# Later loads for the fifth and sixth groups and a new hand-written order in an mLSTM, SoLU and top-1 expert kernel

## The chip, the cores and the metric

The kernel runs on one core of one Trainium2 chip. The metric is the device time of one execution in microseconds (us), lower is better.

## The reference

Three stages follow each other on 4 x 768 = 3072 tokens of 320 numbers. First a gated recurrence (mLSTM, 8 heads of 40), then a layer `x @ w_in`, a softmax-weighted activation, a layer norm and `@ w_out`, then one of 8 experts for each token.

```python
for t in range(S):                                   # stage 1, per batch and head
    m_new = np.maximum(f_gate[:, :, t] + m, i_gate[:, :, t])
    C = f_stab * C + i_stab * einsum('bhd,bhe->bhde', vt, kt)
    n = f_stab * n + i_stab * kt
    y[:, :, t] = sigmoid(o_gate) * (C @ qt) / max(|n @ qt|, 1)
h = x @ w_in; e = np.exp(h - h.max(-1)); solu = h * e / e.sum(-1)    # stage 2
x = layernorm(solu) * g_ln @ w_out
idx = argmax(normalize(x) @ normalize(expert_emb).T / tau)           # stage 3
out = gate * (relu(x @ w1[idx]) @ w2[idx])
```

## The kernel before

The tokens are cut into 24 groups of 128 (6 chunks for each of 4 batches). The recurrence is computed by chunks: for each group the scores of queries and keys (`smat`, L626), their product with the values (`pv`, L637), the part carried over from the chunks before (`inter`, L642) and the new state (`smm`, L647). Then follow for each group the gate (`den`, `og`, L654 to L662), the transpose of x (`xtr`, L671), the first layer (`mm1`, L686 to L695), the softmax (`negmax` L699, `expo` L704, `umul` L709), transposes of u (`utr`, L732), the second layer (`mm2`, L748 to L750) and the row for routing.

Products in full precision are made from two rounded halves, so each weight matrix is split on the core into a high and a low part. `w_in` and `w_out` come as 64-bit numbers and are decoded on VectorE first (`dec_in`, `dec_out`, three instructions each, L397 to L399). ScalarE writes the high part (`whi`, L421 and L424; `ohi`, L566), VectorE the low part (`wlo`, L428; `olo`, L569). This decoding, the gates' running maxima (`gmax0` L348, `gsum0` L358, with TensorE's `gls0` L356 and `gx0` L365 around them), the embeddings' product with `w_out` (`wtr` L525, `ep` L538, which gives the routing scores as extra columns of `w_out`) and the first three groups' attention make up the opening, some 48 us. The raw weights share four slots (`raw`), so the third and the fourth fetch of `w_in` wait until the two decodings of `w_out` have freed theirs. Ten pairs of products without use (`fill`, L600) write into the bank `H`, the same that `gls0` writes and `gsum0` reads.

Routing goes by blocks of up to four groups: place in the expert (`pos`, L810), a key (`key`), two one-hot tables for each group made on GpSimd (`okr`, L837 and L839, for the last block on VectorE), and a product of them that inverts the permutation (`invm`, L845). From the inverted table VectorE works out the rows to gather (`col_0` for the two fullest experts, `col_2` and `col_4` for the others, L1037 to L1041). GpSimd gathers the rows of an expert (`xg`, L1118), TensorE transposes them (`xt`, L1129), and the two layers of the expert follow (`m1`, L1157 to L1161; `m2`, L1208 to L1210).

Nothing is scheduled at run time. Every step is entered into a plan with its engine and with what it needs, and a table of numbers (`AT`) gives each step its place: the steps are sorted by their numbers and written out in that order, so each engine's instructions, and SyncE's loads, stand in it. The numbers only order. Loads of queries and keys (`load_q`, L605, 4 buffers) and of keys, values and gates (`load_n`, L612, 4 buffers) are steps of SyncE; at first they wait for nothing but their buffer. ScalarE applies tanh to each group's gates as soon as its own order comes to it (`tprep`, L618), and GpSimd scales the values (`vprep`, L615).

```python
keys = sorted(self.steps, key=at.get)
for k in plan.order():
    plan.steps[k]["fn"]()
```

Of the kernel before, what the change touches and what calls it, by code (L numbers as in the profile page):

```python
# [20 lines left out]
B, H, S, D = 4, 8, 768, 40  # L21
# [38 lines left out]
NFILL = 10  # L60
INP = ((0, 1), (1, 2), (2, 4), (4, 5))
# [157 lines left out]
def moe_kernel(ctx: ExitStack, tc: tile.TileContext, qkT, nat, gates, w_in, w_out, emb, w1, w2, cst, out):  # L219
# [73 lines left out]
    add = plan.add  # L293
# [777 lines left out]
    g = NG - 1  # L1071
# [498 lines left out]
```

## Time and profile before

| | us |
|---|---|
| three runs: median, lowest, highest | 524.79, 520.2, 525.45 |
| the profiled execution | 522.23 |
| its span, first to last instruction | 520.4 |
| TensorE busy in the span | 494.0 |
| VectorE, ScalarE, GpSimd busy | 340.0, 275.0, 203.9 |
| mean granted TensorE clock | 0.985 |

The profile lists, for each engine, when each instruction started, how long it took, how long the engine had been idle before it and which engine or transfer ended that idle time. Consecutive matmuls overlap in it, since a matmul's end is its last result; the distance from one start to the next is what a matmul costs. The granted clock is 1.00 at TensorE's upper level (2.4 GHz) and 0.50 at its lower (1.2 GHz).

### The profile page before, as it was taken

Reading aid. Unit: us, or ns where it says so; the run is one execution under the profiler, and the core shown is the slowest. Engines: PE = TensorE matmul, PEld = TensorE weight load, DVE = VectorE, ACT = ScalarE, POOL = GpSimd, SP = SyncE. Lnnn points to the kernel's source line nnn. Section 1 sums busy time; section 2 is a strip of 40 time slices with the busy share of each in tenths; the row PEclk is TensorE's granted clock in tenths of the full one; section 3 lists DMA queues with packets and bytes.
Section 4 is the critical chain, followed back from the end, with each engine's and each line's share of the span. In section 5 each row is a group of like instructions: output and inputs, shape, how many; then the busy total and the mean of one; then the engine's idle time right before and its main releaser. Section 6 shows DMA issues by size and latency. Waiting matters only on the chain. (4 is left out here: it accounts for less than half of the span.)

```text
span 520.4 us, 14487 instructions
## 1 busy us (share of the span) xinstructions
PE 494.0 (95%) x5925; PEld 452.2 (87%) x5925; DVE 340.0 (65%) x735; ACT 275.0 (53%) x604; POOL 203.9 (39%) x350
## 2 busy tenths in 40 slices
PE   6869999999999999999999899999999999999991
PEld 5747998888899999889898789898999999999991
DVE  5997667777677587677778778677463655485120
ACT  3572555665656556666467565554543644565220
POOL 3221223266246247345315683656172444112021
PEclk9989999999999999999999899999999999999996
DMA  8962233343341253414041412835631861563000
GB/s 300 412 223 81 80 83 120 113 147 111 90 144 46 77 156 121 144 40 143 3 171 44 152 47 96 276 84 193 231 92 44 285 223 64 217 189 121 14 21 31
DMA packets 20139, 68.01 MB, mean 131 GB/s; under 512 B 2658, under 2 KB 6050, under 8 KB 19680
## 3 DMA queue, kind: packets, MB, share of 16 engines
q1 hardware_dynamic: 17120, 58.27, 33.5%
q0 software_dynamic: 2944, 8.73, 5.3%
q8 instruction: 49, 0.80, 0.7%
q14 instruction: 26, 0.21, 0.1%
HBM read 58.31 MB, written 8.72 MB: 129 GB/s over the span
## 5 line engine op out<-in xcount | busy, mean ns | idle before, releaser
L1222 POOL DMA_INDIRECT out_x<-you,sidx x28 | 30.8, 1099 | 95.5 <-ACT you L1215 82.9
L748 PE MATMUL Y<-OH,uh 128*128 128x328 f32 x192 | 63.4, 330 | 0.0
L1190 DVE SCALAR_TENSOR_TENSOR lu<-hpu,uu 128x384 fp32r<-128x384 f32 (+4 forms) x56 | 28.6, 519 | 53.0 <-ACT uu L1184 43.5
L750 PE MATMUL Y<-OH,ul 128*128 128x328 f32 x192 | 60.3, 314 | 0.2 <-DVE ul L740 0.2
L749 PE MATMUL Y<-OL,uh 128*128 128x328 f32 x192 | 60.4, 315 | 0.0
L1208 PE MATMUL ypu<-hr,uu 128*128 128x320 f32 (+4 forms) x192 | 60.1, 313 | 0.0
L1209 PE MATMUL ypu<-lr,uu 128*128 128x320 f32 (+4 forms) x192 | 59.3, 309 | 0.0
L1184 ACT ACTIVATE uu<-hpu 128x384 fp32r<-128x384 f32 (+7 forms) x64 | 30.4, 483 | 52.2 <-PE hpu L1161 40.0
L1109 DVE TENSOR_TENSOR lr<-raw,hr 128x1024 fp32r<-128x1024 f32 (+1 forms) x32 | 43.4, 1355 | 15.1 <-ACT hr L1102 15.1
L1210 PE MATMUL ypu<-hr,lu 128*128 128x320 f32 (+4 forms) x168 | 51.8, 309 | 0.0
L1102 ACT CAST hr<-raw 128x1024 fp32r<-128x1024 f32 (+1 forms) x40 | 45.2, 1134 | 10.5 <-DMA raw<-in_w 9.4
L736 ACT CAST uh<-tpu 128x512 fp32r<-128x512 f32 x48 | 27.7, 586 | 38.7 <-PE tpu L732 38.4
L704 ACT ACTIVATE e<-H,nmx 128x1024 f32<-128x1024 f32 x24 | 26.8, 1117 | 40.2 <-DVE nmx L699 40.2
L1118 POOL DMA_INDIRECT xgr<-ys,gidx x28 | 36.5, 1302 | 27.3 <-issue 8.9
L699 DVE TENSOR_REDUCE nmx<-H 128x1 f32<-128x1024 f32 x24 | 29.4, 1224 | 26.1 <-PE H L695 24.5
L1157 PE MATMUL hpu<-exr,hr 128*128 128x384 f32 (+7 forms) x128 | 43.7, 341 | 0.0
L1158 PE MATMUL hpu<-exr,lr 128*128 128x384 f32 (+7 forms) x128 | 42.5, 332 | 0.0
L1159 PE MATMUL hpu<-exr,hr 128*128 128x384 f32 (+7 forms) x128 | 42.4, 332 | 0.0
L686 PE MATMUL H<-WH,xh 128*128 128x512 f32 x96 | 40.7, 424 | 1.2 <-DVE u L709 1.1
L740 DVE TENSOR_TENSOR ul<-tpu,uh 128x512 fp32r<-128x512 f32 x48 | 32.4, 687 | 12.6 <-ACT uh L736 12.5
L687 PE MATMUL H<-WL,xh 128*128 128x512 f32 x96 | 37.9, 395 | 0.1
L748 PEld LDWEIGHTS Y<-OH,uh 128*128 128x128 f32 x192 | 36.2, 189 | 2.0 <-ACT yr L766 0.2
(230 smaller groups left out, 1351.3 us busy)
## 6 DMA issues: line engine op xcount, KB each, us to landing
qk<-in_qkT SPq DMA_DIRECT2D x24, 512.0 KB, 4.2
raw<-in_w SPq DMA_DIRECT2D x24, 512.0 KB, 4.7
nat<-in_nat SPq DMA_DIRECT2D x24, 484.0 KB, 3.7
raw<-in_w SPq DMA_DIRECT2D x16, 640.0 KB, 5.3
ys<-yr SPq DMA_DIRECT2D x5, 772.0 KB, 5.0
raw<-in_w_out SPq DMA_DIRECT2D x2, 1280.0 KB, 9.3
raw<-in_w_in SPq DMA_DIRECT2D x3, 512.0 KB, 6.4
raw<-in_w_in SPq DMA_DIRECT2D x1, 1024.0 KB, 8.3
```

The lines of the kernel that those rows point to most:

```text
L686: T.matmul(out=o, lhsT=xh[:, kk, :], rhs=WH[:, kk, f], start=(kk == 0), stop=False)
L748: T.matmul(out=yp, lhsT=uh, rhs=OH[:, k, :], start=(k == 0), stop=False)
L749: T.matmul(out=yp, lhsT=uh, rhs=OL[:, k, :], start=False, stop=False)
L750: T.matmul(out=yp, lhsT=ul, rhs=OH[:, k, :], start=False, stop=(k == 7))
L1102: A.copy(out=R.h[i], in_=R.raw[i])
L1109: eng.tensor_tensor(out=R.l[i], in0=R.raw[i], in1=R.h[i].bitcast(F32), op=ALU.subtract)
L1157: T.matmul(out=o, lhsT=R.h[k][:, fs_], rhs=xh[:, k, tk], start=(k == 0), stop=False)
L1158: T.matmul(out=o, lhsT=R.l[k][:, fs_], rhs=xh[:, k, tk], start=False, stop=False)
L1159: T.matmul(out=o, lhsT=R.h[k][:, fs_], rhs=xl[:, k, tk], start=False, stop=False)
L1208: T.matmul(out=yp, lhsT=uh, rhs=hi, start=(f == 0), stop=False)
L1209: T.matmul(out=yp, lhsT=uh, rhs=lo, start=False, stop=False)
L1210: T.matmul(out=yp, lhsT=ul, rhs=hi, start=False, stop=(f == 7))
```

## The change

The four loads of the groups 4 and 5 (counted from 0) now come after `ep` 1, the second half of the embeddings' product with `w_out`. All numbers of the table are replaced, so that steps stand in a new order on every engine. The steps of the opening move most: the loads, GpSimd's memsets (`set_z` ahead of `sets`), a low part of `w_in`, the fills. Behind the opening most steps keep their neighbours or change places with one of them. No instruction is added or removed.

```diff
+LATER = (4, 5)
...
-    "load_q": "30 115 87 359 332 531 908 1069 ...",
+    "load_q": "30 97 80 345 714 694 903 1065 ...",
-    "col_2": "6816",
+    "col_2": "6550",
...
-        add(("load_q", g), "S", lambda g=g, s=s, q=q: load_q(s, qkT[g], q), war=[of("smat", g - nq), of("inter", g - nq)], size=524)
-        add(("load_n", g), "S", lambda g=g, s=s, q=q: load_n(s, nat[g], q), war=[("og", g - nn), of("smm", g - nn), of("pv", g - nn)], size=496)
+        add(("load_q", g), "S", lambda g=g, s=s, q=q: load_q(s, qkT[g], q), after=[("ep", 1)] if g in LATER else (), war=[of("smat", g - nq), of("inter", g - nq)], size=524)
+        add(("load_n", g), "S", lambda g=g, s=s, q=q: load_n(s, nat[g], q), after=[("ep", 1)] if g in LATER else (), war=[("og", g - nn), of("smm", g - nn), of("pv", g - nn)], size=496)
```

The line numbers of the changed kernel are one higher throughout.

**SyncE, the loads of the opening.** The number behind `qk` or `nat` is the group. Before, from the second fetch of `w_out` on:

```order
L392 DMA raw_66<-in_w_out 128x2560
L605 DMA qk4_260<-in_qkT 128x1024
L605 DMA qk3_270<-in_qkT 128x1024
L314 DMA cs_75<-in_cst 128x496
L612 DMA nat2_321<-in_nat 128x968
L392 DMA raw_66<-in_w_in 128x2048
L612 DMA nat4_431<-in_nat 128x968
L605 DMA qk5_469<-in_qkT 128x1024
L392 DMA raw_66<-in_w_in 128x1024
L612 DMA nat5_504<-in_nat 128x968
```

Now, from the same fetch on:

```order
L393 DMA raw_66<-in_w_out 128x2560
L613 DMA nat2_253<-in_nat 128x968
L606 DMA qk3_269<-in_qkT 128x1024
L613 DMA nat3_276<-in_nat 128x968
L393 DMA raw_66<-in_w_in 128x2048
L393 DMA raw_66<-in_w_in 128x1024
L606 DMA qk5_554<-in_qkT 128x1024
L613 DMA nat4_558<-in_nat 128x968
L606 DMA qk4_561<-in_qkT 128x1024
L613 DMA nat5_567<-in_nat 128x968
```

The four loads of the groups 4 and 5 moved behind the last fetch of `w_in`, and the constants' second part (`cs`) moved out of this stretch, ahead of the second fetch of `w_in`.

**VectorE and TensorE around the gates' second maximum.** VectorE before, from the end of the second decoding of `w_in` to the first decoding of `w_out`:

```order
L399 SCALAR_TENSOR_TENSOR wf0_210<-raw_66,wf0_210 128x512
L492 RECIPROCAL et_125<-et_125 8x1
L493 TENSOR_TENSOR et_125<-et_125,rtau_79 8x1
L358 SCALAR_TENSOR_TENSOR gx_118<-H0_161,z_119 32x767
L631 TENSOR_TENSOR Pt1_242<-S0_1_224,cs_75 128x512
L631 TENSOR_TENSOR Pt1_242<-S1_1_225,cs_75 128x512
L397 TENSOR_SCALAR of0_256<-raw_66 128x1280
```

Now:

```order
L400 SCALAR_TENSOR_TENSOR wf0_211<-raw_66,wf0_211 128x512
L493 RECIPROCAL et_125<-et_125 8x1
L494 TENSOR_TENSOR et_125<-et_125,rtau_79 8x1
L429 TENSOR_TENSOR WL_111<-wf0_211,WH_110 128x512
L359 SCALAR_TENSOR_TENSOR gx_118<-H0_160,z_119 32x767
L632 TENSOR_TENSOR Pt1_243<-S0_1_222,cs_75 128x512
L632 TENSOR_TENSOR Pt1_243<-S1_1_223,cs_75 128x512
L398 TENSOR_SCALAR of0_255<-raw_66 128x1280
```

A low part of `w_in` (L429), which stood behind the gate of group 1, now stands ahead of the maximum (L359). TensorE before, from the last scores of group 1 to the first values:

```order
L626 MATMUL S1_1_225<-qk1_179 128x128
L501 MATMUL tpe_236<-cs_75,en_124 128x8 x2
L501 MATMUL tpe_236<-cs_75,en_124 64x8
L600 MATMUL H0_161<-cs_75 128x128 x4
L365 MATMUL gx_249<-cs_75,gx_118 128x64 x6
L439 MATMUL wd4_262<-wf2_171,cs_75 64x512 x2
L441 MATMUL wd4_262<-WH_110,negi_122 64x512 x2
L637 MATMUL num0_274<-nat0_214,Pt0_198 32x41 x32
```

Now:

```order
L627 MATMUL S1_1_223<-qk1_176 128x128
L601 MATMUL H0_160<-cs_75 128x128 x8
L366 MATMUL gx_245<-cs_75,gx_118 128x64 x6
L502 MATMUL tpe_259<-cs_75,en_124 128x8 x2
L502 MATMUL tpe_259<-cs_75,en_124 64x8
L440 MATMUL wd4_264<-wf2_170,cs_75 64x512 x2
L442 MATMUL wd4_264<-WH_110,negi_122 64x512 x2
L638 MATMUL num0_278<-nat0_215,Pt0_201 32x41 x32
```

The embeddings' transposes (L502) went behind `gx0`; the pair of fill products that stood between `gls0` and the scores of group 1 went behind these scores, and so did a pair that stood later, so that eight fill products (L601) stand ahead of `gx0` instead of four.

**TensorE and GpSimd at the fifth inversion.** `ip4` is its product, `ohr4_0` and `ohv4_0` are the one-hot tables of the block's first group, and Y21 is the second layer of group 21. TensorE before:

```order
L749 MATMUL Y21_4757<-OL_113,uh21_0_4727 128x328
L750 MATMUL Y21_4757<-OH_112,ul21_0_4738 128x328
L845 MATMUL ip4_4781<-ohv4_0_4695,ohr4_0_4693 128x192
L845 MATMUL ip4_4781<-ohv4_1_4725,ohr4_1_4723 128x192
L845 MATMUL ip4_4781<-ohv4_2_4774,ohr4_2_4772 128x192
L845 MATMUL ip4_4781<-ohv4_3_4746,ohr4_3_4744 128x192
L748 MATMUL Y21_4757<-OH_112,uh21_1_4729 128x328
L749 MATMUL Y21_4757<-OL_113,uh21_1_4729 128x328
```

Now:

```order
L750 MATMUL Y21_4760<-OL_113,uh21_1_4722 128x328
L751 MATMUL Y21_4760<-OH_112,ul21_1_4731 128x328
L846 MATMUL ip4_4797<-ohv4_0_4728,ohr4_0_4726 128x192
L846 MATMUL ip4_4797<-ohv4_1_4757,ohr4_1_4755 128x192
L846 MATMUL ip4_4797<-ohv4_2_4779,ohr4_2_4777 128x192
L846 MATMUL ip4_4797<-ohv4_3_4695,ohr4_3_4693 128x192
L733 MATMUL tpu22_0_4810<-cs_75,u22_4802 128x128 x4
```

The four products of the inversion moved behind the second half of Y21, that is behind 12 more matmuls. GpSimd before:

```order
L837 TENSOR_SCALAR ohr4_0_4693<-cs_75,vr4_4684 128x128
L839 TENSOR_SCALAR ohv4_0_4695<-cs_75,vr4_4684 128x192
L837 TENSOR_SCALAR ohr4_1_4723<-cs_75,vr4_4684 128x128
L839 TENSOR_SCALAR ohv4_1_4725<-cs_75,vr4_4684 128x192
L837 TENSOR_SCALAR ohr4_3_4744<-cs_75,vr4_4684 128x128
L839 TENSOR_SCALAR ohv4_3_4746<-cs_75,vr4_4684 128x192
L837 TENSOR_SCALAR ohr4_2_4772<-cs_75,vr4_4684 128x128
L839 TENSOR_SCALAR ohv4_2_4774<-cs_75,vr4_4684 128x192
L723 TENSOR_SCALAR nmx21_4618<-nmx21_4618 128x1
L724 TENSOR_TENSOR nmx21_4618<-nmx21_4618,pw_78 128x1
L725 TENSOR_SCALAR nmx21_4618<-nmx21_4618 128x1
```

Now:

```order
L838 TENSOR_SCALAR ohr4_3_4693<-cs_75,vr4_4684 128x128
L840 TENSOR_SCALAR ohv4_3_4695<-cs_75,vr4_4684 128x192
L838 TENSOR_SCALAR ohr4_0_4726<-cs_75,vr4_4684 128x128
L840 TENSOR_SCALAR ohv4_0_4728<-cs_75,vr4_4684 128x192
L724 TENSOR_SCALAR nmx21_4618<-nmx21_4618 128x1
L725 TENSOR_TENSOR nmx21_4618<-nmx21_4618,pw_78 128x1
L726 TENSOR_SCALAR nmx21_4618<-nmx21_4618 128x1
L838 TENSOR_SCALAR ohr4_1_4755<-cs_75,vr4_4684 128x128
L840 TENSOR_SCALAR ohv4_1_4757<-cs_75,vr4_4684 128x192
L838 TENSOR_SCALAR ohr4_2_4777<-cs_75,vr4_4684 128x128
L840 TENSOR_SCALAR ohv4_2_4779<-cs_75,vr4_4684 128x192
```

The three short instructions of group 21's layer norm (`nmx21`) moved from behind the eight one-hot tables into their middle.

## Rows read from the trace of the kernel before

**Rows 1.** The page's first part: busy us, share, instructions of each engine.
```profile
PE 494.0 (95%) x5925; PEld 452.2 (87%) x5925; DVE 340.0 (65%) x735; ACT 275.0 (53%) x604; POOL 203.9 (39%) x350
```

**Rows 2.** Waits of TensorE, whole span: us in total, times, longest.
```profile
PE txr L1129 <- DMA xgr<-ys,gidx: 2.2, 3, 1.1
...
PE ip L845 <- POOL ohv L839: 1.9, 1, 1.9
PE H L686 <- DVE u L709: 1.1, 1, 1.1
```

**Rows 3.** A stretch of the opening: busy us by engine, granted clock, DMA share, GB/s.
```profile
30.00:35.00 5.00, 4.34 (x52) 2.76 (x51) 4.91 (x6) 2.75 (x10) 0.74 (x1) 0.66 0.88 311
```

**Rows 4.** Timeline of VectorE, opening: start us, us, instruction, idle before it.
```profile
14.40 1.75 DVE L358 TENSOR_TENSOR_SCAN gx<-H,z 32x767 f32<-32x767 f32 x1 [0.48 <-PE H L600]
...
17.39 0.82 DVE L397 TENSOR_SCALAR of<-raw 128x1280 int32<-128x1280 int32 x1
...
19.77 1.91 DVE L399 SCALAR_TENSOR_TENSOR of<-raw,of 128x1280 int32<-128x1280 int32 x1
...
30.43 0.68 DVE L428 TENSOR_TENSOR WL<-wf,WH 128x512 fp32r<-128x512 f32 x1
...
35.38 0.43 DVE L397 TENSOR_SCALAR wf<-raw 128x512 int32<-128x512 int32 x1 [0.19 <-DMA raw<-in_w_in]
```

**Rows 5.** Timeline of TensorE, opening.
```profile
14.30 1.16 PE L626 MATMUL S<-qk 40*128 40x128 f32 x16
...
16.21 1.16 PE L600 MATMUL H<-cs 128*128 128x128 f32 x8 [0.50 <-DVE gx L358]
...
20.45 0.82 PE L637 MATMUL num<-nat,Pt 128*32 128x41 f32 x64
...
30.54 0.43 PE L647 MATMUL stc<-nat 128*32 128x41 f32 x16 [1.90 <-issue]
...
35.92 1.00 PE L538 MATMUL wep<-wt,enT 128*32 128x128 f32 x24 [1.05 <-ACT wt L530]
```

**Rows 6.** Timeline of ScalarE, opening.
```profile
13.71 0.62 ACT L421 CAST WH<-wf 128x512 fp32r<-128x512 f32 x1 [2.99 <-DVE wf L399]
...
45.49 1.12 ACT L704 ACTIVATE e<-H,nmx 128x1024 f32<-128x1024 f32 x1 [5.47 <-DVE nmx L699]
```

**Rows 7.** DMA issues from 15.5 to 16 us: size, us to landing.
```profile
nat<-in_nat SPq DMA_DIRECT2D x1, 484.0 KB, 12.1
```

**Rows 8.** DMA issues from 28.9 to 30 us.
```profile
raw<-in_w_in SPq DMA_DIRECT2D x1, 512.0 KB, 6.4
```

**Rows 9.** Stretches after the fifth inversion: TensorE busy us, granted clock, DMA, GB/s.
```profile
292.00:294.00 2.00, 1.82 (x11) 0.87 0.86 293
294.00:296.00 2.00, 2.00 (x10) 0.50 0.48 195
296.00:298.00 2.00, 2.00 (x11) 0.77 0.00 0
```

**Rows 10.** Timeline of GpSimd at the fifth inversion.
```profile
283.38 0.63 POOL L837 TENSOR_SCALAR ohr<-cs,vr 128x128 fp32r<-128x128 f32 x1 [0.74 <-DVE rt L803]
...
289.84 1.29 POOL L837 TENSOR_SCALAR ohr<-cs,vr 128x128 fp32r<-128x128 f32 x1
...
292.21 0.19 POOL L723 TENSOR_SCALAR nmx<-nmx 128x1 f32<-128x1 f32 x1
...
293.17 0.27 POOL L725 TENSOR_SCALAR nmx<-nmx 128x1 f32<-128x1 f32 x1
```

**Rows 11.** Timeline of TensorE at the fifth inversion and at the second expert's gathers.
```profile
292.18 0.47 PE L845 MATMUL ip<-ohv,ohr 128*128 128x192 f32 x2 [1.89 <-POOL ohv L839]
292.49 0.34 PE L748 MATMUL Y<-OH,uh 128*128 128x328 f32 x1
...
292.81 0.31 PE L750 MATMUL Y<-OH,ul 128*128 128x328 f32 x1
...
331.46 0.81 PE L1129 MATMUL txr<-cs,xgr 112*128 112x112 f32 x6 [1.12 <-DMA xgr<-ys,gidx]
```

230 rows, old and new, of the table AT are left out of this document.

## Prediction

> **What bounds the kernel.** I read the page's first part first. TensorE is busy 494.0 us of the 520.4 [rows 1], and the matmuls are the same in both kernels, so only its idle time (26.4 us) and the stretches at its lower clock level can change. The list of TensorE's waits then says where idle time can be moved: 2.2 us for gathered rows, 1.9 us for a one-hot table, 1.1 us for the first softmax product (L709, `umul` 0), which ends the opening [rows 2]. The last of these is the end of a VectorE chain. In the opening VectorE is 98% busy (4.91 of 5.00) while TensorE has gaps [rows 3], and VectorE's own rows show waits of only 0.48 and 0.19 us from the maximum at 14.40 on [rows 4]. So VectorE's queue sets when the opening ends; loads and TensorE matter there only where they make VectorE wait. Behind the opening TensorE's queue sets the end.
>
> **Loads.** The four deferred loads (2 MB) used to stand partly ahead of the last fetch of `w_in`, which landed 6.4 us after its issue [rows 8]; VectorE waited 0.19 us for it [rows 4]. That wait is all that earlier landing can give: **-0.2**. The constants' second part (0.25 MB) now stands ahead of `w_out`; at 311 GB/s [rows 3] that is 0.8 us later at most, and VectorE comes to `w_out` 0.6 us later (below) and did not wait there before, so 0 to +0.2; I take 0.
>
> **VectorE and TensorE around 14 to 25 us.** The low part L428 (0.68 us long, 0.6 from start to start) moves from 30.43 to ahead of the maximum `gsum0`. It needs ScalarE's high part, which ends at 13.71 + 0.62 = 14.33 [rows 6]. So it runs from 14.4 and `gsum0` starts at 15.0 instead of 14.40: +0.6 there, -0.6 again at 30.43. The earlier wait of 0.48 was for a fill that is no longer ahead, so nothing more is lost.
>
> `gsum0` then ends at 15.0 + 1.75 = 16.75. The fills write the bank that it reads, and the row before shows that they wait for it (0.50 us until 16.21) [rows 5]. Group 1's scores, 1.16 us from 14.30 before, now come without the pair of fills in front (half of the 1.16 of two pairs, some 0.5), so they end near 14.9. TensorE then has nothing until 16.8: an idle time of 1.9 us where it had 0.50.
>
> From the fills to the first values (`pv` 0) TensorE took 20.45 - 16.21 = 4.24 us. Now eight more fill records stand there (1.16 us as eight did, 1.1 without the last one's drain) and the embeddings' transposes (which filled 15.46 to 15.71 before, 0.25). So `pv` 0 starts at 16.8 + 4.24 + 1.1 + 0.25 = 22.4, ends at 23.2, and group 2's scores, of the same form as the 1.16, end at 24.3 [rows 5]. VectorE starts `w_out`'s decoding at 17.39 + 0.6 = 18.0 and ends it at 19.77 + 1.91 + 0.6 = 22.3 [rows 4]. Next are the gate's three short instructions (an estimate of 0.7 together) and the product with group 2's scores, which could start at 23.0 and instead waits until 24.3: **+1.3**. With +0.6 - 0.6 - 0.2 the opening ends 1.1 us later, if TensorE's clock stays at its upper level.
>
> **Does the clock fall?** Before, the clock stood at 0.66 between 30 and 35 us, behind an idle time of 1.90 us that ended at 30.54 [rows 3, 5], and at 0.87, 0.50 and 0.77 from 292 to 298 us behind one of 1.89 [rows 9, 11]; behind 1.05 and 1.12 no row shows a loss. The new idle time of 1.9 is like the two that were followed by a fall. A fall cost 5 x 0.34 = 1.7 us of work in the first case, 2 x (0.13 + 0.50 + 0.23) = 1.7 in the second. All of it would lie on the way to `pv` 0 and group 2's scores, and VectorE would wait 3.0 instead of 1.3. I take it: opening **+2.8**; bounds +1.1 (no fall) and +2.8.
>
> **Deferred loads, other end.** ScalarE's order puts the tanh of groups 4 and 5 ahead of the first `expo`, which started at 45.49 [rows 6]. `ep` 1 ended at 35.92 + 1.00 [rows 5]; four issues and a landing of 6.4 us [rows 8] end at 36.9 + 1.5 + 6.4 = 44.8, inside 45.49 (both ends move with the opening). Hidden, 0; the cover is 0.7 us. With the longest landing of the opening, 12.1 [rows 7], the last would come at 50.5, 5.0 us too late.
>
> **The fifth inversion, near 290 us.** TensorE came to it with two products at about 290 and waited 1.89 us until 292.18 for GpSimd's last one-hot table [rows 11], whose making ended as the next instruction began, at 292.21 [rows 10]. Now 12 matmuls stand ahead; two of them are 0.32 apart (292.49 to 292.81), so 12 take 1.9 us and TensorE comes 1.9 us later. But GpSimd's three instructions for group 21 (292.21 to 293.44, 1.23 us) now stand ahead of the last two tables, which end 1.23 us later. The wait becomes 1.89 - 1.9 + 1.23 = 1.2 to 1.3: **-0.6**. That is nearer the 1.12 us behind which the clock held than the 1.89 behind which it fell, so I also take the 1.7 us of the fall as gained: **-1.7** (bounds 0 and -1.7).
>
> The one-hot instruction L837 took 0.63 us first and 1.29 last [rows 10]. The Trainium skill (GPSIMD Engine Reference, Key points) says that GpSimd shares its SBUF interfaces with VectorE and contends with VectorE's instructions that have two SBUF inputs. By it a table set would cost 0.63 + 1.00 where no such instruction runs, four 6.5 us instead of 8.8, the wait would be gone, and the sum 1.2 us lower. The trace bears out that the same instruction doubles; that VectorE causes it, no row shows. I keep 8.8, since VectorE's splits of expert weights stand in that stretch in both orders.
>
> **Gathers, 324 to 356 us.** TensorE waited three times, 2.2 us in all [rows 2], 1.12 of it at 331.46 [rows 11]. In the new order the seventh inversion comes one block of eight expert matmuls earlier (at the 0.16 of [rows 11], at least 1.3 us), so the rows for the first wait are gathered 1.3 us earlier: it goes. The other two belong to the third expert, whose row numbers (`col_2`) VectorE now works out right behind the experts' ranking instead of behind the small unit's first layer: they go too. But each gather after the fifth needs a buffer freed by an earlier landing, and the third expert's first transposes also stand earlier; I keep 0.5 us of new waits: **-1.7**, bounds 0 and -2.2.
>
> **Sum.** +2.8 - 0.6 - 1.7 - 1.7 = -1.2 us. The profiled execution took 522.23 us (520.4 of span, the rest around it unchanged), so it would take 521.0. The median shown is 524.79 and the runs go from 520.2 to 525.45; the four times together have a mean of 523.2, and I set the 1.2 us off against that: **522.0**.
>
> **Rivals.** *A, the clock holds in the opening* (idle time shorter, or the two falls had another cause): opening +1.1, the rest as above, -2.9 in all: 520.3. For it: no row shows what decides a fall. Against: both idle times of 1.9 were followed by one. *B, the middle gains nothing*: the wait at the fifth inversion stays long enough for a fall, and gathers are late again, since their buffers chain them; only the opening's loss is left: 523.2 + 2.8 = 526.0. For it: GpSimd gets 1.23 us more ahead of the table; against: TensorE's 1.9 us later arrival. *C, slower by the deferral*: the sixth group's tanh holds up ScalarE ahead of the first `expo`, with the 12.1 us landing 5.0 us, 522.0 + 5.0 = 527.0. It decides from a landing behind 45.5 us on; against it, the queue is empty then, and 12.1 was seen with other loads ahead. That the deferral does nothing for the time either way is part of the forecast (-0.2).
>
> **How the numbers follow.** Chances: forecast 0.42, A 0.27, B 0.24, C 0.07. Leaving out C and the outer tails of A and B, and with the spread of the runs shown (2.6 us about their middle), the range is 518.0 to 526.5; the forecast's own is 520.0 to 524.0. A measurement of this kernel can tell about 1% from no change. Against 524.79, faster by over 1% means below 519.5: part of A and a low draw of the forecast, 0.17. Slower means above 530.0: C and a high draw of B, 0.06. Within 1%: 0.77.
>
> **What would show it.** In the changed profile: `gsum0` at 15.0; TensorE idle some 1.9 us ahead of the fills, and a granted clock under 1.00 between 17 and 21 us; VectorE waiting for TensorE ahead of group 2's product (L632) by 1 to 3 us; the last `w_in` decoding without a wait; the first `expo` some 2.8 us after 45.49; the wait for L840 at about 1.2 us with the clock at 1.00 behind it; no wait for gathered rows over 0.5 us. The forecast is wrong if the fills do not wait for `gsum0`, if tanh of group 5 ends behind the first `negmax`, or if TensorE waits at a place that the list of waits before does not have.

## The result and the profile after

| kernel | median us | executions | profiled execution, us | its span, us |
|---|---|---|---|---|
| before | 525.45 (520.2 to 525.92) | 11 | 522.23 | 520.4 |
| after | 519.86 (519.14 to 521.93) | 11 | 519.58 | 517.8 |

The ratio of after to before is 0.9913, with a 95% interval of 0.9889 to 0.9938: 0.9% less, which is within the 1% that the prediction called no change, and inside its range (518.0 to 526.5), though close to the edge of both: the medians alone are 5.6 us apart, 1.1%. The two profiled executions are 2.65 us apart. The gap between the two differences is what most of the experiments are about.

The page's first part for after, which answers [rows 1], has TensorE 1.2 us less busy with the same 5925 records:

```profile
PE 492.8 (95%) x5925; PEld 451.1 (87%) x5925; DVE 339.9 (66%) x735; ACT 273.7 (53%) x604; POOL 199.7 (39%) x350
```

The list of TensorE's waits of after answers [rows 2] (us in total, times, longest). No row for gathered rows is left, and the wait at the inversions is down from 1.9 to 1.2:

```profile
PE stc L648 <- issue: 2.3, 1, 2.3
PE S L627 <- DMA qk<-in_qkT: 1.7, 1, 1.7
...
PE ip L846 <- POOL ohv L840: 1.2, 1, 1.2
```

VectorE's timeline of after, opening, answers [rows 4]: the low part of `w_in` (L429) does stand ahead of the second scan (`gsum0`, L359), but the scan starts at 15.92 and not at 15.0, since the first scan (L349) already waited 1.81 us for the gates. The gate's three instructions and the product with group 2's scores wait 1.61 and 0.38 us. The profile puts the first of these waits down to ScalarE's `WH`, but `den` reads `num`, and TensorE's products of `num` ended at 24.24 us:

```profile
9.55 1.75 DVE L349 TENSOR_TENSOR_SCAN gx<-gt 32x768 f32<-32x768 f32 x1 [1.81 <-DMA gt<-in_gates]
...
15.08 0.69 DVE L429 TENSOR_TENSOR WL<-wf,WH 128x512 fp32r<-128x512 f32 x1 [0.44 <-ACT WH L422]
15.92 1.75 DVE L359 TENSOR_TENSOR_SCAN gx<-H,z 32x767 f32<-32x767 f32 x1
...
24.38 0.17 DVE L655 SCALAR_TENSOR_TENSOR den<-num,gw 128x8 f32<-128x8 f32 x1 [1.61 <-ACT WH L451]
...
25.36 1.29 DVE L632 TENSOR_TENSOR Pt<-S,cs 128x512 f32<-128x512 f32 x2 [0.38 <-PE S L627]
```

TensorE's timeline of after answers [rows 5]. The first two gate products (L357, 512 columns each) take 1.91 us together and the later two of the same size 1.02; the idle time ahead of the fills at 17.72 is 0.75 us, not 1.9:

```profile
8.52 1.16 PE L627 MATMUL S<-qk 40*128 40x128 f32 x16 [1.70 <-DMA qk<-in_qkT]
9.61 0.92 PE L601 MATMUL H<-cs 128*128 128x128 f32 x4
10.32 1.91 PE L357 MATMUL H<-gt,cs 128*128 128x512 f32 x2
12.03 1.70 PE L357 MATMUL H<-gx,cs 128*128 128x512 f32 x2
13.56 1.02 PE L357 MATMUL H<-gx,negi 128*128 128x512 f32 x2
...
17.72 2.05 PE L601 MATMUL H<-cs 128*128 128x128 f32 x16 [0.75 <-DVE gx L359]
```

Stretches of after (TensorE busy us, granted clock, DMA share, GB/s): the lower clock comes at 10 to 15 us, behind the 1.70 us wait for the first queries, and behind 15 us, to 22.5, the column has 1.00:

```profile
10.00:12.50 2.50, 2.50 (x6) 0.50 1.03 412
12.50:15.00 2.50, 2.50 (x7) 0.82 1.08 441
```

Stretches of after behind the fifth inversion, which answer [rows 9] (0.87, 0.50 and 0.77 there), stay at 1.00:

```profile
295.50:297.50 2.00, 1.94 (x14) 1.00 0.87 350
297.50:299.50 2.00, 2.00 (x11) 1.00 0.02 6
```

TensorE's timeline of after at the fifth inversion answers [rows 11]:

```profile
294.01 0.36 PE L846 MATMUL ip<-ohv,ohr 128*128 128x192 f32 x2
295.56 0.47 PE L846 MATMUL ip<-ohv,ohr 128*128 128x192 f32 x2 [1.18 <-POOL ohv L840]
```

### The profile page after: what moved, and what is told of

Read it like the earlier page. It is cut to its first block, busy times and chain, and to the rows that moved or that the text cites. A ratio compares the mean times of both kernels' runs of the same rounds, so it can differ in the third digit from the quotient of the medians.

```text
span 517.8 us, 14480 instructions
## 1 busy us (share of the span) xinstructions
PE 492.8 (95%) x5925; PEld 451.1 (87%) x5925; DVE 339.9 (66%) x735; ACT 273.7 (53%) x604; POOL 199.7 (39%) x350
## 5 line engine op out<-in xcount | busy, mean ns | idle before, releaser
L1223 POOL DMA_INDIRECT out_x<-you,sidx x28 | 29.3, 1046 | 92.5 <-ACT you L1216 76.2
L1119 POOL DMA_INDIRECT xgr<-ys,gidx x28 | 30.4, 1086 | 24.4 <-issue 11.7
```

## The experiments

The next table is worked out from TensorE's and VectorE's timelines of all the profiles but a_tail's. "Ahead of scores" is the wait for the first queries, "scan" the start of `gsum0` on VectorE. A runs from the span's start to the scores of the 22nd of the 24 groups, B from there to the sixth inversion's first product, C from there to the start of the last matmul. So A holds the opening, B the fifth inversion, C the expert stage.

| kernel | ahead of scores | scan | A | B | C | time of it |
|---|---|---|---|---|---|---|
| before | 0.93 | 14.40 | 243.43 | 70.26 | 195.76 | 522.23 |
| b_look1 | 1.86 | 17.92 | 248.26 | 70.24 | 195.72 | 526.61 |
| b_warm | 0.76 | 14.92 | 246.67 | 68.65 | 197.16 | 524.82 |
| b_inv | 0.7 | 13.91 | 244.19 | 67.85 | 196.66 | 521.76 |
| a_open | 1.8 | 16.01 | 245.69 | 68.66 | 198.43 | 525.21 |
| after | 1.70 | 15.92 | 245.52 | 68.28 | 193.09 | 519.58 |
| after2 | 2.0 | 17.43 | 246.41 | 68.24 | 193.59 | 520.69 |
| c2_act16 | 2.1 | 16.30 | 246.07 | 68.25 | 193.48 | 520.42 |
| c2_back | 2.4 | 18.15 | 247.23 | 68.25 | 198.00 | 525.91 |
| b_open | 1.03 | 16.26 | 245.94 | 68.24 | 197.59 | 524.22 |
| b_open16 | 1.3 | 16.03 | 246.05 | 68.31 | 196.92 | 523.98 |
| a_warm | 1.0 | 15.59 | 245.39 | 68.23 | 198.86 | 525.27 |
| no_later | 2.2 | 17.56 | 247.34 | 68.22 | 195.36 | 523.45 |

**b_look1: before once more.** The same kernel, to see where its usual execution loses 3 us against the profiled one.

> The kernel before, unchanged, for a second profile. Its median over 11 executions is 525.4 us, its profiled execution took 522.2. Theory 1 (the usual execution loses the 3.5 us in the middle part, where before has idle times of 1.9 us followed by a lower granted clock): if this execution is near 525.5, one or two more stretches of 10 us show a granted clock below 0.95 than in the first profile, and the rest of the trace is alike within 0.5 us. Rival (the loads of the opening come late, as in the kernel after): the first scores land 0.5 us or more later and all behind them is moved by 1 to 3 us.

This execution took 526.61 us, beside a median of 524.92 for 25 executions of before. B and C are those of the first profile within 0.04 us; A is 4.83 us longer, which is more than all of the 4.38 us between the two executions. Theory 1 falls and its rival stands, though what is behind the scores moved by more than its 1 to 3 us. TensorE's timeline of b_look1, to be held against [rows 5]:

```profile
3.05 3.78 PE L600 MATMUL H<-cs 128*128 128x128 f32 x16 [3.05 <-DMA cs<-in_cst]
8.69 2.08 PE L626 MATMUL S<-qk 40*128 40x128 f32 x16 [1.86 <-DMA qk<-in_qkT]
10.70 1.22 PE L600 MATMUL H<-cs 128*128 128x128 f32 x4
11.71 1.91 PE L356 MATMUL H<-gt,cs 128*128 128x512 f32 x2
13.42 1.87 PE L356 MATMUL H<-gx,cs 128*128 128x512 f32 x2
15.12 1.02 PE L356 MATMUL H<-gx,negi 128*128 128x512 f32 x2
```

TensorE's timeline of before, the first fills:

```profile
3.17 3.76 PE L600 MATMUL H<-cs 128*128 128x128 f32 x16 [3.17 <-DMA cs<-in_cst]
```

VectorE's timeline of b_look1, with the second scan that starts at 14.40 in [rows 4]:

```profile
17.92 1.75 DVE L358 TENSOR_TENSOR_SCAN gx<-H,z 32x767 f32<-32x767 f32 x1 [3.12 <-PE H L600]
```

The queries came 0.83 us later than in the first profile (8.69 against 7.86), and behind the longer wait the scores took 2.08 us where [rows 5] has 1.16 for the same form, and two gate products 1.91. VectorE then waited 3.12 us for them. The rows do not show a clock that fell behind this wait: sixteen fills took 3.76 to 3.78 us ahead of it in both profiles, where sixteen later in after take 2.05. So TensorE began at its lower level in both; by the first scores it had risen in the first profile, and in b_look1 the first products at the upper rate are those at 15.12. So the profile on which the prediction was built was a quick execution of before, in the very stage whose cost it put highest.

**b_open and a_open: the openings exchanged.** b_open is after with all steps ahead of `mm1` (2, 0), the third group's first product, in before's order and without the deferral. a_open is before with after's order up to the same place. (The recorded text calls this product the fifth group's; it is the fifth step of its kind. All steps are numbered anew in the two tables; the order alone counts.)

```diff
-LATER = (4, 5)
+LATER = ()
 AT = {
...
-    "gsum0": "264",
...
+    "gsum0": "38",
...
```

> The order of before up to the fifth group's first product, without the deferral of groups 5 and 6's loads, and the order of after from there on. Theory (the opening of after costs 2.1 to 2.9 us and the fifth inversion and the gathers pay it back twice over): the middle of the program starts where before starts it, the wait for the fifth inversion's matrix is 1.2 us and not 1.9, so 519.9 - 2.1 to 2.9 = 517.0 to 517.8 us. Rival 1 (the loss in the opening is given back later anyway, since group 6's start is set by loads): 519.0 to 520.5. Rival 2 (what after gains comes from the opening's order in the executions that are not profiled): 523 to 525.

> The order of after up to the fifth group's first product, loads in its order too but without the explicit wait, and the order of before from there on. Theory (opening alone costs 2.1 to 2.9 us, nothing else is changed): before + 2.1 to 2.9, so 527.5 to 528.3 where before's median is 525.4, or 524.3 to 525.1 against its profiled 522.2; the wait for the fifth inversion's matrix stays at 1.7 to 2.0 us with a lower granted clock behind it. Rival 1 (given back later): 525.0 to 526.0. Rival 2 (the opening is what gained): 519 to 521.

b_open: 524.32 us (ratio to before 0.9993, 0.9963 to 1.0023). a_open: 525.16 (0.998, 0.9954 to 1.0007). Neither sum of parts holds: before's opening with after's remainder ought to have been the quickest, and is as slow as before. The table says why. b_open has no quicker opening than after (A 245.94 against 245.52): its first scores come at 7.86 us as in before's first profile, but they take 2.08 us, as in b_look1, and the scan starts at 16.26. And it loses 4.5 us in C, where its order is after's. a_open has B of 68.66 with before's order of the fifth inversion. TensorE's timeline of a_open there:

```profile
294.44 0.47 PE L845 MATMUL ip<-ohv,ohr 128*128 128x192 f32 x2 [1.90 <-POOL ohv L839]
```

A stretch of a_open behind it:

```profile
296.40:298.40 2.00, 2.00 (x16) 1.00 0.38 156
```

The wait is the 1.89 of [rows 11] again, and yet the clock behind it stays at 1.00. The fall of [rows 9] is there in two of four profiles with this order (before and b_look1, B 70.2; not in a_open and b_warm, B 68.65), and is worth their difference, 1.6 us. In C a_open waits 2.4 us for one set of gathered rows, where before waited 1.1 at most; TensorE's timeline of a_open:

```profile
355.63 0.69 PE L1129 MATMUL txr<-cs,xgr 128*128 128x128 f32 x2 [2.38 <-DMA xgr<-ys,gidx]
```

**c2_back: is it the constants' second part that delays the first queries?**

```diff
-    "ld_c2": "60",
+    "ld_c2": "346",
...
-    "mku": "170",
+    "mku": "520",
```

> The kernel after with the second part of the constants loaded late again, where before has it (behind w_out's second piece), and the product that needs it moved back with it. Theory (0.25 MB of constants in small rows ahead of queries and keys hold up the first scores by 0.7 us, VectorE's first maximum comes 0.7 us later, and the clock falls at 10 to 15 us behind the 1.7 us wait): the first scores are back at 7.9 us from 8.5, the wait ahead of them at 0.9 to 1.0 from 1.7, the clock at 10 to 15 us above 0.9, the opening 0.7 to 2.4 us shorter, the time 517.5 to 519.2. Rival (something else in the order of loads holds up queries and keys): scores still at 8.5, the time within 0.5 of after's 519.9.

524.56 us (0.9989, 0.9957 to 1.0021). The theory falls: the first scores came at 9.22 us, later still. In all profiles they start between 7.46 and 9.22 us. With before's order of loads five profiles (before, b_look1, b_open, b_open16, b_inv) have a mean of 8.01, with after's four (after, after2, a_open, no_later) 8.75. The order thus seems to cost some 0.7 us there, but not by this load. What was not expected is C, 4.9 us longer than after's. ScalarE's timeline of c2_back:

```profile
341.23 0.52 ACT L1216 ACTIVATE you<-ypu,xgater 128x320 f32<-128x320 f32 x1
345.20 0.25 ACT L1166 COPY hsu<-hpu 128x112 f32<-128x112 f32 x1 [3.45 <-remote]
```

ScalarE's timeline of after at the same place:

```profile
339.48 0.52 ACT L1216 ACTIVATE you<-ypu,xgater 128x320 f32<-128x320 f32 x1
340.04 0.25 ACT L1166 COPY hsu<-hpu 128x112 f32<-128x112 f32 x1
```

The copy needs a result that TensorE had finished before 341.7, and it starts at 345.20. The profile names no releaser that it knows. TensorE waits from 344.06 on for 1.75 us, and its matmuls of 432 columns then take 0.56 us each, against 0.36 in after. b_open has the same stall, 2.76 us long, at the same instruction.

**after2, and c2_act16: is the stall a matter of the place in ScalarE's program?** after2 is after, unchanged. c2_act16 is c2_back with 16 one-element copies on ScalarE at 3 us, where it is idle.

```diff
+    def dum():
+        dmy = tl("sg", [1, 1], "dmy")
+        for _ in range(16):
+            A.copy(out=dmy, in_=prep["onef"][:1, :1])
+
+    add("dum", "A", dum, after=["sets"])
```

> The kernel after, unchanged, beside the other kernels of this group, with a second profile. Theory 1 (the last part of the order of after stands without a stall in every execution; c2_back and b_open, which have the same last part, lost 4.5 us at 344 us while ScalarE waited 2.8 to 3.5 us ahead of a copy): 519 to 522 us again, no ScalarE wait of over 1.2 us between 335 and 350 us, 193 us from the sixth inversion's product to the end. Theory 2 (the stall comes at random in any execution): some executions near 524, and it may show in the profile. The first scores land between 7.8 and 9.3 us in all profiles so far whatever the order of loads, and a wait of over 1 us ahead of them halves the granted rate of the matmuls behind it; after's opening then ends within 1.5 us of where it ended in the first profile.

> The kernel c2_back with 16 copies of one element on ScalarE at 3 us, where ScalarE is idle until 9.9 us. They change no other engine's work; every later instruction of ScalarE stands 16 places further in its program. Theory A (the 3.45 us stall of ScalarE at 342 us depends on the place of that copy in ScalarE's program, at its 390th row or so): it is gone or moved to an instruction 16 places earlier, and without it the time is 4.5 us shorter, 520 to 521. Theory B (it depends on what the DMA queues and GpSimd do at that time): it stays where it is, 524 to 526.

after2: 519.9 us (0.9912, 0.9885 to 0.9939; 518.7 to 521.17 in 10 executions, beside 524.91 for 31 of before). C is 193.59 and there is no stall, so after's time stands. Its A is 246.41, 0.9 more than in its first profile. c2_act16: 519.77 (0.9904, 0.9877 to 0.993), no stall, C 193.48. That is what theory A expected. The next group of runs took it down again, and c2_act16 differs from c2_back in more than the copies, as shown there.

**b_open16 and a_warm.** b_open16 is b_open with the same 16 copies. a_warm is after with two more fills ahead of the first scores, which adds nothing on ScalarE:

```diff
-NFILL = 10
+NFILL = 12
...
-    "fill": "62 79 96 114 154 271 282 291 300 519",
+    "fill": "62 79 96 114 122 126 154 271 282 291 300 519",
```

> The kernel b_open (opening of before, without the deferral; the rest of after) with 16 copies of one element on ScalarE at 3 us, where ScalarE is idle. Theory (b_open's 524.3 is after's time plus the stall of ScalarE at 342 us, which costs 4.5 us and hangs on the place of the copy in ScalarE's program; the two openings cost the same on the average): no stall, 519.3 to 520.3 us. Rival 1 (before's opening is 2 to 3 us faster than after's once the stall is gone): 516.5 to 518. Rival 2 (16 places do not remove this stall): 524.

> The kernel after with two more fills ahead of the first scores, as b_warm had them. Theory (behind the wait of 1.7 to 2.0 us for the first queries the gates' products run at half rate in part, and the second scan starts at 15.9 or 17.4 us): products at 0.43 us, the scan at 15.2 to 15.9, limited by the low part of w_in ahead of it; 0.3 to 1.5 us under after's 519.9, so 518.4 to 519.6. Rival (what is won is lost again at the stalls near 32 and 41 us, or the further instructions bring a stall of ScalarE as in c2_back): 519.9 to 521, or 524.

b_open16: 523.62 us (0.9963, 0.9931 to 0.9994), with a stall of 3.44 us at the same copy. a_warm: 523.05 (0.9952, 0.9924 to 0.998), with one of 3.47. ScalarE's timeline of a_warm:

```profile
339.44 0.52 ACT L1216 ACTIVATE you<-ypu,xgater 128x320 f32<-128x320 f32 x1
343.42 0.25 ACT L1166 COPY hsu<-hpu 128x112 f32<-128x112 f32 x1 [3.47 <-remote]
```

In a_warm ScalarE's program is after's, and 16 places changed nothing in b_open16. So the place in ScalarE's program is not the cause.

The record shows what goes with the stall. It names chip 6 for b_look1, b_open, a_open and c2_back, chip 7 for after2, b_warm, b_inv and c2_act16, chip 0 for b_open16, a_warm, no_later and a_tail, and none for the first profiles of before and after. Of the eight profiles with after's expert stage, the five with the stall are all from the chips 6 and 0, and after2 and c2_act16, which are free of it, from chip 7. before shows no such difference: its medians on the three chips are 524.92, 524.91 and 524.66 us.

The traces differ in the same way, whatever the kernel: those of the chips 6 and 0 hold 4284 to 4498 updates of semaphores, the other six, before's and after's first among them, 4704 to 4735. Between 325 and 350 us the five with the stall hold 173 to 188, after, after2 and c2_act16 456 to 459. (An update is the signal by which one engine releases another.) In the five, TensorE's updates for ScalarE come 1.4 to 1.6 us apart at the stall. In c2_back they are at 343.67, 345.12 and 346.57 us, by their order for matmuls that ended at 341.03, 341.61 and 342.31, and the two copies start 0.08 us behind the last two; in after each lies within 0.02 us of its matmul's end. So the copy waits for a late signal from TensorE. Whether the chip, the recording of the execution or something else makes it late is not shown, since after itself has no run on the chips 6 and 0. It does not seem to come in every execution there: the quickest of c2_back, a_warm and b_open16 took 520.65, 520.4 and 519.8 us.

In the opening a_warm did what was expected: scan at 15.59, A the smallest of all kernels with after's opening (245.39), but only 0.1 to 1.0 us less than after's two. The version that was to beat after is 3 us slower in a group with the stall, where after was not run. TensorE's timeline of a_warm also has an idle time ahead of the fills of the length that the prediction gave to after:

```profile
17.39 2.05 PE L601 MATMUL H<-cs 128*128 128x128 f32 x16 [1.87 <-DVE gx L359]
```

The sixteen fills behind it take the same 2.05 us as in after behind 0.75 us: here an idle time of 1.87 us was followed by no fall.

**b_warm: does keeping TensorE busy ahead of the first scores hold its clock?** The same two fills in before.

```diff
-NFILL = 10
+NFILL = 12
...
-    "fill": "62 79 96 114 154 251 289 298 419 477",
+    "fill": "62 79 96 114 122 126 154 251 289 298 419 477",
```

> The kernel before with two more fills (8 records of matmuls on the identity, about 1.9 us) ahead of the first scores, so that TensorE does not stand idle while it waits for the first queries. Theory (in two of the three profiles with before's opening the 512-column products for the gates took 0.86 us each and not 0.43 behind a wait of 1.0 to 1.9 us, and the second scan started at 16.3 and 17.9 us and not at 14.4): the products take 0.43 us, the scan starts at 14.4 to 15.6 us, and the median falls by 1 to 3 us from before's, to 522 to 524. Rival (the clock falls for another reason, or the time lost there is caught up later): the scan starts at 16 us or later, or the median is within 0.7 us of before's.

523.21 us (0.9972, 0.9936 to 1.0007). TensorE's timeline of b_warm:

```profile
8.68 1.16 PE L626 MATMUL S<-qk 40*128 40x128 f32 x16 [0.76 <-DMA qk<-in_qkT]
9.77 0.71 PE L600 MATMUL H<-cs 128*128 128x128 f32 x4
10.32 1.02 PE L356 MATMUL H<-gt,cs 128*128 128x512 f32 x2
```

VectorE's timeline of b_warm:

```profile
14.92 1.75 DVE L358 TENSOR_TENSOR_SCAN gx<-H,z 32x767 f32<-32x767 f32 x1 [0.48 <-PE H L600]
```

The products take 1.02 us a pair and the scan starts at 14.92, though the scores start as late as in b_look1. That part of the theory fits, in one execution; before and b_inv have the same 1.02 us without the two fills, with queries that came at 7.86 and 7.46. But of the ten profiles of the table whose queries came at 8.18 us or later, only b_warm and a_warm had no slow gate products. The median is 1.7 us under before's, with an interval that takes in no change. Not all of the 3.0 us between the scans of b_look1 and b_warm is kept: their A differ by 1.6.

**b_inv: the fifth inversion alone.**

```diff
-    "invm": "2527 3376 4228 5112 5772 6221 6381",
+    "invm": "2527 3376 4228 5112 5790 6221 6381",
```

> The kernel before with one step moved: the fifth inversion's product behind the second half of group 22's second product, as in after. Theory (step 5 of the prediction, 0.6 to 0.7 us of the wait and 1.7 us of lower clock behind it): the wait ahead of the product falls from 1.9 to 1.2 us, the clock stays at 1.00 behind it, and the distance from group 24's first scores to the sixth inversion's product falls by 2.4 us; the median 2.0 to 2.8 us under before's. Rival (the clock's fall is not due to this wait): the wait is shorter by 0.7 us, and that is all, 0.5 to 0.9 us under before's.

523.19 us (0.9988, 0.9949 to 1.0026). B is 67.85: 2.4 us less than in before and b_look1, 0.8 less than in a_open and b_warm, which had the wait without the fall. The median is 1.7 us under before's, between what the two theories expected, with an interval that takes in no change. TensorE's timeline of b_inv shows the wait gone altogether, and one of 1.31 us for the next softmax product 10 us later in its place:

```profile
292.49 0.92 PE L845 MATMUL ip<-ohv,ohr 128*128 128x192 f32 x4
...
303.04 0.41 PE L732 MATMUL tpu<-cs,u 128*128 128x128 f32 x2 [1.31 <-DVE u L709]
```

**no_later: after without the deferral.**

```diff
-LATER = (4, 5)
+LATER = ()
...
-    "load_q": "30 97 80 345 714 694 ...",
+    "load_q": "30 97 80 345 335 531 ...",
...
-    "load_n": "219 124 315 372 704 728 ...",
+    "load_n": "219 124 315 372 499 587 ...",
```

> The kernel after without the deferral: the loads of groups 5 and 6 carry no wait for the product with w_out and stand in SP's queue where before has them, so they start at 15 to 30 us. Everything else as in after. Theory (step 1 of the prediction, the deferral is worth 0.2 us): within 0.5 us of after, 519.4 to 520.4, last w_in waited for by 0.2 to 0.5 us. Rival 1 (it is the deferral that holds the opening's loads on time): 521 to 523, with the wait ahead of the first queries or of w_out's decoding longer by over 1 us. Rival 2 (a stall of ScalarE by a changed program): 524, seen as a wait of ScalarE of over 2 us near 342 us.

523.66 us (0.9992, 0.9967 to 1.0018). It does not decide the deferral. C is 1.8 to 2.3 us longer than after's by a short form of the stall (the copy waited 2.07 us), and A is 0.9 to 1.8 longer than in after's two profiles. The wait for the first gates is 2.98 us there against 1.81 and 2.24, but c2_back, which has the deferral, has nearly the same A. VectorE decodes the last `w_in` without a wait, as it does in after.

**a_tail: the expert stage in before's order.** After's order up to the fifth inversion, before's behind it.

> The kernel after up to the fifth inversion, and the order of before behind it (gathers, sixth and seventh inversion, experts). Theory (step 6 of the prediction; after has 193.1 and 193.6 us from the sixth inversion's product to the end, profiles with before's order 195.7 to 198.4, by waits for gathered rows of 2.0 to 3.6 us in all): 2.0 to 3.5 us over after, 522 to 523.5, waits for gathered rows back at 2 to 3.6 us. Rival (after's gain in the last part comes from the shift of ScalarE's program alone): within 0.7 us of after.

524.8 us. The mixed order also changed part of what the expert stage computes, so I take nothing from its time. Its waits for gathered rows, 2.4 us in two, are the kind that before's order has and after's has not.

## Why the prediction was right, and where it was not

- **What bounds.** TensorE is 95% busy in after, and VectorE's chain through the scans still sets the opening: A minus the scan's start lies between 229.0 and 231.8 in every profile, while the scan itself moves by 4.2 us. No run changed this chain alone.
- **Loads.** 0 for the constants' second part agrees with c2_back, whose opening is no shorter without it. The last `w_in` is decoded without a wait, as said, but so it is in no_later, while c2_back, with the deferral, waits 0.29 us for it: the 0.2 was not the deferral's. Whether the deferral does something else for the opening is open.
- **Opening, +2.8.** This is the step that failed. In the pair of profiles group 1's first product comes 2.86 us later (50.96 against 48.10), of which 2.1 are left at the 22nd group. But the make-up was another one: `gsum0` 1.5 us later, not 0.6, as queries and gates landed later; 0.75 us of idle time ahead of the fills, not 1.9; the lower clock at 10 to 15 us, not 17 to 21; 2.0 us of waits ahead of group 2's product, not 3.0. And as a statement on the kernels it was far too large. A with before's opening (before, b_look1, b_inv, b_open, b_open16) has a mean of 245.6 and goes from 243.4 to 248.3; with after's (after, after2, a_open) 245.9, from 245.5 to 246.4. The new opening costs some 0.3 us on the average, which the spread of 4.8 us within the first five does not tell from nothing, and not 2.8, since the profile I took for before was the quickest of the five. The 1.7 us for the clock had no firm ground either: a_warm has the idle time of 1.9 us, and no fall behind it.
- **Tanh of groups 4 and 5.** Hidden, as said: the first `expo` started at 48.03, 2.54 us after the 45.49 of [rows 6], behind VectorE's maximum and not behind a tanh. Rival C did not come.
- **Fifth inversion, -0.6 and -1.7.** The wait is 1.18 us and the clock behind it 1.00, both as forecast. Inside it two errors cancel: GpSimd's three instructions for group 21 took 2.7 us and not 1.23 (288.87 to 291.59, one of them 1.71), and the four tables some 7.3 us, not 8.8 (285.58 to 295.59, less the 2.7). Of the Trainium skill's rule on shared interfaces (GPSIMD Engine Reference, Key points) no run here shows whether VectorE was the cause. The 1.7 for the clock was too sure: the fall is there in two of four profiles with the old order. On the average B falls from 69.45 to 68.25, by 1.2 us and not by 2.3.
- **Gathers, -1.7.** All waits for gathered rows are gone, none of the 0.5 us that I kept. The price was too low: with before's expert stage TensorE waits 2.0 to 3.6 us for them (b_look1, before, b_inv, a_open, b_warm), and C has a mean of 196.8 against 193.4 without the stall with after's: 3.4 us. Chip 7 alone, where both were run without the stall, gives the same (b_warm and b_inv 196.9, after2 and c2_act16 193.5). On chip 6 the stall takes it all back (b_look1 and a_open 197.1, b_open and c2_back 197.8). That the clock or other waits of that stage make up the part beyond the waits was not taken apart.
- **Sum.** By the means, +0.3 - 1.2 - 3.4 = -4.3 us, where the medians of the second comparison differ by 5.0. The forecast's -1.2 came from a base that was quick where the change loses and ordinary where it gains. Setting it off against the mean of four times (523.2) took back only a part of this. That after lands at 519.9 in 21 executions is also due to the stall at 342 us not coming: the five kernels with its expert stage that ran on the chips 6 and 0 show it and have medians of 523.05 to 524.56 us, 0.1 to 0.5% under before's. So a gain of 0.9% is shown for the runs of the result and for chip 7 alone. That the time fell within 1% of before's was in part luck: 1% is 5.2 us here, and the measured change is some four times the -1.2 of the forecast, whose own stretch (520.0 to 524.0) the 519.86 just misses. The opening was priced 2.5 us too high, the gain at the inversion 1.1 us too high and that of the gathers 1.7 us too low, and neither the stall nor the spread of the opening was in the sum.
- **Rivals.** A (opening 1.1, 520.3) came nearest to the time. At the place that it meant its condition held (0.75 us of idle time, the clock at 1.00 behind it), but the clock was low earlier in the opening, from 10 to 15 us, and it was the gathers that brought the time down. B's doubt on the fall was half right, its doubt on the gathers wrong.

What stays open: why TensorE's signals come late at 342 us on the chips 6 and 0, and what time after has there; how much the deferral does; which load holds up the first queries. No version here beats both kernels: c2_act16, at 519.77, is no different from after.

## What to carry to other kernels

Profile the kernel before more than once and compare the profiles stage by stage before pricing a change: here one stage of the same kernel differed by 4.8 us, more than any part was priced at (2.8 at most) or measured at (3.4). Price a clock fall by the share of executions in which it comes, and read it from the length of equal instructions. Exchange whole stages between two versions to learn which gains, but check what the rest of the trace does, and run both parents beside the exchanged versions on the same chip: here a stall that went with the chip could be taken for the doing of an edit 300 us away.

## What the runs showed of the hardware that I had not expected

- **Equal waits, different clocks.** Behind the same wait of 1.86 to 1.90 us at the same product the clock fell in two of four profiles, and behind one of 1.87 us in a_warm's opening it did not. Ahead of the first scores, waits of 0.7 to 1.0 us were followed by matmuls at full rate (scores in 1.16 us). Behind waits of 1.3 to 2.1 us in after, a_open, c2_act16 and b_open16 the scores took 1.16 us and slow gate products came later, from 9.8 to 10.8 us on.
- **A clock that rises at another time in each execution.** In b_look1, b_open, after2, c2_back and no_later the first scores took 2.08 us, and no product reached the upper rate before 12.5 us. The sixteen fills ahead of them took 3.8 us, as at the lower level of 1.2 GHz, in these as in before (3.76). The Trainium skill (TensorE: Matmul & The Clock Gate, Part 1: The HAM clock gate) says that the number of slow matmuls at a start changes from run to run for the same kernel; before and b_look1 agree, with scores of 1.16 and 2.08 us in the same program, and so do after and after2.
- **The clock column shows 1.00 where it has no record.** In b_look1 two products took 1.91 and 1.87 us from 11.71 on, as at the lower level, and in after 1.91 from 10.32 on. After's row has 0.50 there, but b_look1's has 1.00. The first record of the clock in b_look1's trace is at 15.11 us, in after's at 6.55, and the column has 1.00 ahead of it in both, also where the first fills run slowly. Stretches of b_look1:

```profile
10.00:12.50 2.50, 2.50 (x13) 1.00 1.07 426
12.50:15.00 2.50, 2.50 (x4) 1.00 1.00 419
```

- **A signal that comes late.** One copy on ScalarE started 2.1 to 3.5 us after its operand was there, in the five kernels with after's expert stage that ran on the chips 6 and 0, whose C is 2.0 to 5.5 us over the 193.4 of those without the stall. TensorE's updates for ScalarE came 1.4 to 1.6 us apart there, in traces that lack over half of the updates that the others hold between 325 and 350 us.
